# Value products in three blocks per head pair instead of four, and a staggered inversion of the softmax sums

## The chip, the core and the metric

The kernel runs on one core of one Trainium2 chip. The core has a matrix engine (PE, with weight loads shown as PEld), a vector engine (DVE), an activation engine (ACT), a general engine (POOL) and a queue engine (SP) that here issues all DMAs. The metric is the device time of one execution in microseconds (us). Lower is better.

## The reference

One layer over 2048 positions of width 640: a normalized input goes through sliding-window attention (32 heads of width 20, window 256) and, beside it, through a wide layer of 1536 with a squared ReLU; the results are multiplied.

```python
xn = _layernorm(x)                                   # x: 1 x 2048 x 640
qkv = (xn @ wqkv).reshape(B, S, 3, H, Dh)            # H = 32, Dh = 20
scores = einsum("bhqd,bhkd->bhqk", q, k) * Dh**-0.5
mask = (i - j >= 0) & (i - j < 256)
p = softmax(where(mask, scores, -1e9))
s = einsum("bhqk,bhkd->bhqd", p, v) ... @ wo
h = relu(xn @ w1 + b1) ** 2
g = silu(h @ w2 + b2)
return x + s * g
```

## The kernel before

All float32 products are split into a rounded high part and a remainder, and three products of the parts are added up. Contractions over 128 rows of the filler work are cut into two halves of 64 rows, which PE can run side by side on the two halves of its array.

A first stage (to about 139 us) normalizes x, transposes it, and makes the values (v) and the first group of queries and keys. Then comes the main stage: 16 pairs of heads, each with 16 tiles of 128 positions, gives 256 steps and some more at the end (`steps = NP * NT + LAG + PLAG`). A step `s` does, for a pair `p`:

- `scores` (PE, L479; tile `sps`) for tile `s`, from which DVE takes row maxima (L487); every fourth step the maxima of four tiles are turned on PE and sent by a small DMA (`mrow`, L504) into two further rows of the queries `qs`.
- `scores_t` (PE, L519; tile `stps`) for tile `s - LAG` (LAG is 9): the scores transposed, for one tile of keys and the three tiles of queries that see it, with the maximum subtracted through the `mrow` rows; ACT takes the exponential (L525, tile `p`) and POOL clears what lies outside the window (L526, L528). The result stays in one of 8 buffers.
- every fourth step, `values` (PE, L547; tile `ops`): the exponentials of four key tiles times the values, in a block. The last product of a block is PLAG = 2 steps behind its exponentials. A product uses all 128 rows and 32-column strips of the array: two heads and even and odd query tiles in four strips, with 21 columns each, the 21st being a column of ones that gives the softmax sum. The bank `ot` holds four columns of 128, so eight query tiles at a time.
- after a block, `evac` copies two columns to `osb` (ACT, L552) and a DMA stores them (`o<-osb`), 0.8 us later on the planner's clock, into `o_d[g]`, one buffer for each of the four groups `g` of query tiles.

What fills PE between these is one long list of other products, the `filler`: the remaining queries and keys (`qkps`), the wide layer's first product (`hps`) and second (`yps`), and last the output projection (`wops`). `fill` gives out filler until a planner's clock has reached the step's due time; the clock adds a constant for each product (`COST`, and `PV` for a block of values), and `pace` spreads the whole over the steps. DMAs are issued by SP in the order in which the code writes them; loads of x for the wide layer (`xb`), of the next pair's queries and keys, and stores are handed out by `issue` and `post_all` in each step.

The last stage: `wops` needs the attention output divided by the softmax sums. `invert` loads the sums of a group (`rec<-o`, L1064) once the last pair's block has been stored (`stored(g)`), inverts them (DVE, L1066) and stores them (L1067); `load` fetches the outputs (`ob<-o`, L1107) and the inverses (`sums<-rec`, L1108); `turn_out` multiplies them (DVE, L1123) and splits them. `late` calls these in the last blocks of `yps`.

Of the kernel before, what the change touches and what calls it, by code (L numbers as in the profile page):

```python
# [9 lines left out]
F32 = mybir.dt.float32  # L10
F32R = mybir.dt.float32r
BF16 = mybir.dt.bfloat16
AF = mybir.ActivationFunctionType
ALU = mybir.AluOpType

P = 128
# [5 lines left out]
NT = S // P  # L22
KC = D // P
NP = H // 2
NB = 4
BT = S // NB
# [4 lines left out]
HALF = D // 2  # L31
NFH = F // 2 // P
WIDE = 2
FHALF = F // 2
MT = 256
LAG = 9
# [4 lines left out]
WARM2 = 10  # L41
COST = {P: 0.067, 2 * P: 0.12, HALF: 0.147, 3 * P: 0.172, BT: 0.23}
SCALE = DH ** -0.5
PV = 1.57
PLAG = 2
NEG = -1.0e30
EPS = 1e-5
SETTLE = 0.45
# [10 lines left out]
def attn_mlp_kernel(ctx: ExitStack, tc, x, wqkv, wo, w1, b1, w2, b2, out):  # L59
    nc = tc.nc  # L60
# [25 lines left out]
    o_d = [dram.tile([NP, P, MT], F32, name=f"o_{g}") for g in range(NB)]  # L86
# [326 lines left out]
    at2 = ctx.enter_context(tc.tile_pool(name="at2", bufs=2))  # L413
# [9 lines left out]
    clock = [0.0, 0.0, 0.0]  # L423
# [106 lines left out]

    ot = po_.tile([P, 4, P], F32, tag="o", name="ops")

    def values(p, g):
        for kb in range(4 * g, 4 * g + 4):
            pt = pts.pop((p, kb))
            ts = range(kb, min(kb + 3, NT))
            same, other = [t for t in ts if t % 2 == kb % 2], [t for t in ts if t % 2 != kb % 2]
            parts = [same] if kb % 8 < 6 else [[t] for t in same]
            for part in parts + [other]:
                for hh in range(2):  # L540
                    if not part:
                        continue
                    t = part[0]
                    r0 = 32 * (2 * hh + t % 2)
                    c0 = t // 2 % 4
                    first = t % 8 < 2 and kb == max(0, t - 2) or kb == 0
                    nc.tensor.matmul(ot[r0:r0 + VW, c0:c0 + len(part), :], vps[p][:, kb // 4, kb % 4, hh, :], pt[:, hh, :].rearrange("p (t n) -> p t n", n=P)[:, t - kb:part[-1] - kb + 1:2, :], start=first, stop=part[0] == kb, skip_group_check=True)  # L547
        clock[:2] = [max(clock[:2]) + PV] * 2

        def evac():  # L550
            osb = at2.tile([P, 2, P], F32, tag="osb", name="osb")
            nc.scalar.activation(osb, ot[:, 2 * g % 4:2 * g % 4 + 2, :], AF.Copy)  # L552
            post(o_d[g][p], osb.rearrange("p e n -> p (e n)"), 0.8)
        later(SOON, evac)


    state = [0.0, 0.0, 0]
# [3 lines left out]
    def post(dst, src, wait=0.0, then=lambda: None):  # L561
        def go():
            posts.append((dst, src))
            then()
        if whole[0] or not wait:
            go()
        else:
            later(wait, go)

    def post_all():  # L570
        for dst, src in posts:
            nc.sync.dma_start(dst, src)
        posts.clear()
# [9 lines left out]
    def later(wait, fn):  # L583
        tasks.append((clock[0] + wait, len(tasks), fn))
# [274 lines left out]
    def filler():  # L859
# [6 lines left out]
        for g, b in order_qk:  # L866
# [9 lines left out]
            for w in "qk":  # L876
                hi, lo = (t() for t in ws[g][w])
# [35 lines left out]
        def late():  # L913
            j = lates[0]
            lates[0] += 1
            if j >= 3:
                load(0)
            if j >= 4:
                load(1)
            if j >= 6:  # L920
                turn_out(0, 0)
            if j >= 7:
                turn_out(0, 1)
                load(2)
# [120 lines left out]
        return 4 * (u // 2) + u % 2 + 2 * t2  # L1045

    def stored(g):
        return NP * NT - NT + 4 * g + 3 + LAG + PLAG

    rec_d = [dram.tile([2, H, MT], F32, name=f"rec_{g}") for g in range(NB)]  # L1050
    recs = {}

    lates = [0]

    def invert():
        for g in range(NB):
            over = state[2] >= 10 ** 6
            if not over and state[2] < stored(g) + 3:
                return
            if g not in recs:  # L1060
                rows = o_d[g].rearrange("p (h r) n -> (p h) r n", h=2)
                recs[g] = at2.tile([P, P], F32, tag="rec", name="rec")
                for par in range(2):
                    nc.sync.dma_start(recs[g][64 * par:64 * (par + 1)], rows[:, 32 * par + DH].rearrange("h (j n) -> h j n", n=P))  # L1064
            elif recs[g] is not None and (state[2] >= stored(g) + 5 if not over else True):
                nc.vector.reciprocal(recs[g], recs[g])  # L1066
                nc.sync.dma_start(rec_d[g].rearrange("a h (j n) -> (a h j) n", n=P), recs[g])  # L1067
                recs[g] = None

    def room_of(tag, name):  # L1070
        if tag == "p32":
            return at2.tile([P, 2, 3 * P], F32, tag="p32", bufs=8, name=name).rearrange("p a n -> p (a n)")[:, :D]
        return wgt.tile([P, D], F32, tag=tag, name=name)
# [24 lines left out]
    def load(u):  # L1098
        if u in ld or u >= 2 * NB or recs.get(u // 2, 0) is not None:
            return  # L1100
        if u % 2 == 0:
            obs[u // 2] = bigp.tile([P, KC * BT], F32, tag="big", name=f"ob_{u // 2}")
        ob = obs[u // 2][:, u % 2 * 2 * D:(u % 2 + 1) * 2 * D].rearrange("p (c n) -> p c n", c=KC)
        sums = at2.tile([P, MT if u // 2 % 3 == 0 else BT], F32, tag=("sums", "relu", "sq")[u // 2 % 3], name="sums")[:, :MT]
        rows = o_d[u // 2].rearrange("p (h r) n -> (p h) r n", h=2)[:, 32 * (u % 2):32 * (u % 2) + VW]
        for k in range(4):
            nc.sync.dma_start(ob[32 * k:32 * k + H], rows[:, k:DH:4])  # L1107
        nc.sync.dma_start(sums, rec_d[u // 2][u % 2].unsqueeze(0).to_broadcast([4, H, MT]))  # L1108
        ld[u] = (ob, sums)
# [86 lines left out]

    fl = filler()
    steps = NP * NT + LAG + PLAG
    pace = (8 * (KC - 1) * 15 * COST[BT] + 2 * NB * (15 * (WIDE * COST[BT] + 2 * (NFH - WIDE) * COST[MT]) + 8 * 18 * COST[HALF]) + NP * (2 * NT * COST[3 * P] + NB * PV)) / (steps - 1)

    def fill(upto):
        soon()
        while clock[0] < upto:
            c = next(fl, None)
            if c is None:
                clock[0] = upto
                soon()
                return
            if whole[0]:
                clock[:2] = [clock[0] + c] * 2  # L1210
            soon()

    with tc.manual_schedule(engines={E_.PE, E_.Activation, E_.DVE, E_.Pool, E_.SP}):
        load_v(0)
        nc.vector.memset(ot, 0.0)
        loads = []

        def at_step(n):
            return divmod(n, NT) if 0 <= n < NP * NT else None

        for s in range(steps):
            state[2] = s
            vload[0] = 0.2 * (s % 4 == 0) + 0.5 * (s % 4 == 3)
            post_all()
            invert()
            if s >= NP * NT - NT + LAG + 2:
                fetch_y()
            issue(RATE)
            a, b, e = (at_step(s - lag) for lag in (0, LAG, LAG + PLAG))
            if a:  # L1230
                p, q = a
                if q == 0:
                    ensure_bulk(loads)
                if s == 2:
                    ones_rows(1)
                if q == 2 and p < NP - 1:
                    assert made_for(p + 1, 0)
                    loads = [bulk_dma(0.7, *l) for l in pair_loads(p + 1, 0)]
                if q == LAG and p < NP - 1:
                    assert made_for(p + 1, 1)  # L1240
                    loads += [bulk_dma(0.7, *l) for l in pair_loads(p + 1, 1)]
                if q == LAG + 4 and p < NP - 1:
                    load_v(p + 1)
            rows = None
            if a:
                sc = scores(p, q)
            if b:
                stp = scores_t(*b)
            if s % 4 == 0 and 0 < s <= NP * NT:
                rows = max_rows((s - 1) // NT, (s - 1) % NT // 4, stp[0] if b else pair_tile())  # L1250
            if a:
                maxima(*a, *sc)
            if b:
                exps(*b, *stp)
            if rows:
                rows()
            fill((s + EARLY_FILL) * pace)
            post_all()
            issue(RATE)
            flush()  # L1260
            tick()
            if e and e[1] % 4 == 3:
                fill((s + 1) * pace - PV)
                values(e[0], e[1] // 4)
            else:
                fill((s + 1) * pace)
        finish()
        post_all()
        state[2] = 10 ** 6
        for _ in fl:  # L1270
            post_all()
            flush(mark() - 1)
        flush()
        post_all()
# [23 lines left out]
```

## Time and profile before

| | |
|---|---|
| median of 3 runs | 859.34 us (858.82 to 859.89) |
| profiled execution, its own time | 859.53 us |
| its span | 857.8 us |
| granted PE clock, mean | 0.997 |
| DVE, ACT, POOL busy | 54%, 49%, 38% |
| main stage with blocks of values | about 139 to 776 us of the span |
| output projection | 782.9 to 853.5 us |

The profile records one execution. Rows of groups give line, engine, operation, output and inputs with their sizes, the number of instructions, then busy time in us and the mean of one in ns, then the idle time ahead of them with what ended it. Rows of the timeline give start, duration, engine, line and a number of merged instructions. In the trace each value product is two instructions.

### The profile page before, as it was taken

The page shows a single profiled execution, that of the slowest core. Times are in us where ns is not written, and L with a number is a line of the kernel's source. Part 1 is how long each engine was busy: PE and PEld are TensorE (multiplying, and loading weights), DVE is VectorE, ACT ScalarE, POOL GpSimd, SP SyncE. Part 2 cuts the span into 40 slices and gives each one's busy share as a digit, 9 for nine tenths or more (in the row PEclk, how much of TensorE's full clock was granted, in tenths as well). Part 3 has the DMA queues.
Part 4 walks back from the last instruction along what each step waited for, and adds up shares of the span by engine and source line. Part 5 has one row for each costly group of instructions (what it writes and reads, how often), then busy time and mean ns, then how long its engine had stood idle before and what let it go on. Part 6 is the DMA issues. An engine that isn't in the chain of part 4 may idle for free.

```text
span 857.8 us, 25542 instructions
## 1 busy us (share of the span) xinstructions
PE 845.3 (99%) x10160; PEld 786.1 (92%) x10160; DVE 459.1 (54%) x1370; ACT 421.6 (49%) x792; POOL 328.7 (38%) x652
## 2 busy tenths in 40 slices
PE   9999999999999999999999999999999989999998
PEld 8999999888888899999999989999999989999997
DVE  7652136656577545455445466655445444435764
ACT  5222114545556753754654764854754743753321
POOL 6010002334333553553543543643543533541443
PEclk9999999999999999999999999999999999999999
DMA  7997587869889564355266245585376274367992
GB/s 250 327 399 279 170 206 267 263 210 286 278 260 275 146 215 130 84 172 151 77 198 184 61 130 162 144 256 165 77 208 191 61 229 127 126 155 198 277 258 111
DMA packets 94366, 166.42 MB, mean 194 GB/s; under 512 B 10920, under 2 KB 43816, under 8 KB 93224
## 3 DMA queue, kind: packets, MB, share of 16 engines
q1 hardware_dynamic: 94248, 164.80, 63.3%
q8 instruction: 80, 1.31, 0.6%
q14 instruction: 38, 0.31, 0.1%
HBM read 93.66 MB, written 70.52 MB: 191 GB/s over the span
## 4 chain that ended last, share of the span: by engine, by line
PE 93%; DMA 2%; DVE 2%; ACT 1%; issue 1%; SPq 1%; POOL 0%; DVEq 0%
PE hps L469 20%; PE yps L469 20%; PE qkps L469 13%; PE ops L547 10%; PE wops L607 8%; PE vps L229 8%; PE stps L519 5%; PE sps L479 4%; PE qkps L206 3%; PE tps L173 1%; DMA qs<-mrow 1%; DMA qs<-q_d 1%; DMA yin<-y 1%; DVE junk L487 0%; DMA xt<-in_A_x_dram 0%
## 5 line engine op out<-in xcount | busy, mean ns | idle before, releaser
L487 DVE CUSTOM_DVE_ANT_0 junk<-sps,mask 128x384 bf16<-128x384 f32 (+2 forms) x512 | 272.6, 532 | 251.7 <-PE hps L469 70.1
L525 ACT ACTIVATE p<-stps 128x768 f32<-128x768 f32 (+2 forms) x256 | 197.5, 772 | 264.6 <-PE stps L519 216.2
L526 POOL TENSOR_SCALAR_AFFINE_SELECT p<-p 128x256 f32<-128x256 f32 x256 | 107.7, 421 | 332.7 <-ACT p L525 327.8
L469 PE MATMUL yps<-w,hh 64*128 64x320 f32 x1536 | 229.2, 311 | 1.8 <-DVE ysb L996 1.7
L469 PE MATMUL hps<-xb,w 64*128 64x256 f32 (+1 forms) x2100 | 218.6, 305 | 0.0
L469 PEld LDWEIGHTS hps<-xb,w 64*128 64x128 f32 x2100 | 199.2, 187 | 6.2 <-issue 5.1
L469 PEld LDWEIGHTS yps<-w,hh 64*128 64x128 f32 x1536 | 182.2, 186 | 7.5 <-issue 3.4
L469 PE MATMUL yps<-w,hl 64*128 64x320 f32 x768 | 173.5, 310 | 0.0
L479 PE MATMUL sps<-ks,qs 60*128 60x384 f32 (+2 forms) x512 | 141.5, 341 | 1.3 <-DVE mt L487 1.1
L519 PE MATMUL stps<-qs,ks 62*128 62x384 f32 (+2 forms) x512 | 134.5, 332 | 2.4 <-DMA qs<-mrow 2.4
L469 PEld LDWEIGHTS yps<-w,hl 64*128 64x128 f32 x768 | 113.5, 186 | 1.8 <-issue 1.7
L469 PE MATMUL qkps<-xT,wgkh 64*128 64x512 f32 x320 | 100.6, 395 | 0.0
L469 PE MATMUL qkps<-xT,wgqh 64*128 64x512 f32 x320 | 98.1, 392 | 0.0
L528 POOL TENSOR_SCALAR_AFFINE_SELECT p<-p 128x256 f32<-128x256 f32 x224 | 94.1, 420 | 0.0
L547 PE MATMUL ops<-p,vp 128*21 128x128 f32 (+1 forms) x2112 | 92.8, 313 | 0.0
L519 PEld LDWEIGHTS stps<-qs,ks 62*128 62x128 f32 x512 | 87.1, 188 | 3.4 <-issue 2.7
L479 PEld LDWEIGHTS sps<-ks,qs 60*128 60x128 f32 x512 | 85.3, 185 | 4.2 <-DVE mt L487 2.7
L547 PEld LDWEIGHTS ops<-p,vp 128*21 128x21 f32 x2112 | 65.2, 100 | 23.6 <-issue 11.4
L229 PE MATMUL vps<-wv,xT 128*128 128x320 f32 x480 | 71.5, 308 | 0.0
L229 PEld LDWEIGHTS vps<-wv,xT 128*128 128x128 f32 x480 | 70.5, 188 | 0.1
L966 POOL TENSOR_TENSOR hl<-sq,hh 128x512 fp32r<-128x512 f32 x48 | 62.2, 1296 | 19.0 <-ACT sq L965 18.8
L607 PE MATMUL wops<-wo,oT 128*128 128x320 f32 x384 | 61.6, 309 | 0.7 <-DVE ysb L996 0.7
(104 smaller groups left out, 1166.8 us busy)
## 6 DMA issues: line engine op xcount, KB each, us to landing
ks<-k_d SPq DMA_DIRECT2D x64, 240.0 KB
qs<-q_d SPq DMA_DIRECT2D x64, 240.0 KB
xb<-xs SPq DMA_DIRECT2D x60, 256.0 KB
xs<-xT SPq DMA_DIRECT2D x8, 1280.0 KB
k_d<-shm SPq DMA_DIRECT2D x19, 512.0 KB
q_d<-shm SPq DMA_DIRECT2D x19, 512.0 KB
y<-ysb SPq DMA_DIRECT2D x28, 320.0 KB
o<-osb SPq DMA_DIRECT2D x64, 128.0 KB
```

Source lines behind the costliest of these rows:

```text
L206: nc.tensor.matmul(ps, wt[:, c, :], xT[part][b][:, c * BT + t0:c * BT + t0 + n], start=m == 1, stop=m == 3 * KC)
L229: nc.tensor.matmul(ps, xT[xp][b][:, c * BT + t * P: c * BT + (t + 1) * P], wv[wp][:, c, nh * HALF:(nh + 1) * HALF], start=first and m == 0 ...
L469: return nc.tensor.matmul(out, a[r], b_[r], skip_group_check=True, **kw)
L479: nc.tensor.matmul(ss[hh][:, :nk], qs[i][o, q * P:(q + 1) * P], ks[i][o, k0 * P:k0 * P + nk], start=True, stop=True)
L487: nc.vector.tensor_tensor_reduce(out=junk[:, :nk], in0=ss[hh][:, :nk], in1=mask[:, 3 * P - nk:], scale=1.0, scalar=-3.0e38, op0=ALU.add, o ...
L519: nc.tensor.matmul(tps[:, hh, :n], ks[i][o, kb * P:(kb + 1) * P], qs[i][o, kb * P:kb * P + n], start=True, stop=True)
L525: nc.scalar.activation(p32[:, :, :n], tps[:, :, :n], AF.Exp, scale=SCALE)
L526: nc.gpsimd.affine_select(p32[:, :, 0:P], p32[:, :, 0:P], pattern=[[0, 2], [1, P]], compare_op=ALU.is_ge, fill=0.0, base=0, channel_multip ...
L528: nc.gpsimd.affine_select(p32[:, :, 2 * P:], p32[:, :, 2 * P:], pattern=[[0, 2], [-1, P]], compare_op=ALU.is_gt, fill=0.0, base=0, channel ...
L547: nc.tensor.matmul(ot[r0:r0 + VW, c0:c0 + len(part), :], vps[p][:, kb // 4, kb % 4, hh, :], pt[:, hh, :].rearrange("p (t n) -> p t n", n=P ...
L607: nc.tensor.matmul(ps, a, b_, start=j == 0, stop=j == n - 1)
L966: nc.gpsimd.tensor_sub(hh[1][:, :BT], sq, f32(hh[0]))
```

## The change

The 16 key tiles of a pair are cut at 6, 12 and 16 instead of every 4; the blocks stand one step behind the exponentials instead of two, and each has its own cost on the planner's clock. A block's sums leave `ot` as three, three and two columns, in one or two copies where they wrap around, and go to the groups' buffers without the booked delay. In the last stage the inversion takes one group at a time, in one buffer, and waits some calls between its load and the reciprocal; the first loads of outputs start one call later.

```diff
-PV = 1.57
-PLAG = 2
+CUTS = (0, 6, 12, NT)
+PVS = (2.25, 2.25, 1.42)
+PLAG = 1
...
-    def values(p, g):
-        for kb in range(4 * g, 4 * g + 4):
+    def values(p, i):
+        lo, hi = CUTS[i], CUTS[i + 1]
+        for kb in range(lo, hi):
...
-        clock[:2] = [max(clock[:2]) + PV] * 2
+        clock[:2] = [max(clock[:2]) + PVS[i]] * 2
 
         def evac():
-            osb = at2.tile([P, 2, P], F32, tag="osb", name="osb")
-            nc.scalar.activation(osb, ot[:, 2 * g % 4:2 * g % 4 + 2, :], AF.Copy)
-            post(o_d[g][p], osb.rearrange("p e n -> p (e n)"), 0.8)
+            c0, c1 = lo // 2, hi // 2
+            osb = at2.tile([P, 3, P], F32, tag="osb", name="osb")
+            c = c0
+            while c < c1:
+                n = min(4 - c % 4, c1 - c)
+                nc.scalar.activation(osb[:, c - c0:c - c0 + n], ot[:, c % 4:c % 4 + n, :], AF.Copy)
+                c += n
+            for g in range(c0 // 2, (c1 + 1) // 2):
+                d0, d1 = max(c0, 2 * g), min(c1, 2 * g + 2)
+                post(o_d[g][p, :, (d0 - 2 * g) * P:(d1 - 2 * g) * P], osb[:, d0 - c0:d1 - c0].rearrange("p e n -> p (e n)"))
         later(SOON, evac)
...
-            if j >= 3:
+            if j >= 4:
                 load(0)
-            if j >= 4:
                 load(1)
...
     def stored(g):
-        return NP * NT - NT + 4 * g + 3 + LAG + PLAG
+        return NP * NT - NT + min(c for c in CUTS if c >= 4 * (g + 1)) - 1 + LAG + PLAG
...
+    calls, ready = [0], [0]
 
     def invert():
+        calls[0] += state[2] >= 10 ** 6
         for g in range(NB):
             over = state[2] >= 10 ** 6
-            if not over and state[2] < stored(g) + 3:
+            if over and calls[0] < ready[0]:
+                return
+            if not over and state[2] < stored(g) + 2 or over and calls[0] < ready[0]:
                 return
             if g not in recs:
+                if any(r is not None for r in recs.values()):
+                    return
+                ready[0] = calls[0] + 3
...
-                recs[g] = at2.tile([P, P], F32, tag="rec", name="rec")
+                recs[g] = at2.tile([P, P], F32, tag="rec", bufs=1, name="rec")
...
-            elif recs[g] is not None and (state[2] >= stored(g) + 5 if not over else True):
+            elif recs[g] is not None and (state[2] >= stored(g) + 4 if not over else True):
...
                 recs[g] = None
+                ready[0] = calls[0] + 2
...
-            if e and e[1] % 4 == 3:
-                fill((s + 1) * pace - PV)
-                values(e[0], e[1] // 4)
+            if e and e[1] + 1 in CUTS:
+                i = CUTS.index(e[1] + 1) - 1
+                fill((s + 1) * pace - PVS[i])
+                values(e[0], i)
```

More of the change, by code (lines that the diff above doesn't have):

```diff
@@ L1198, in attn_mlp_kernel @@
     steps = NP * NT + LAG + PLAG
-    pace = (8 * (KC - 1) * 15 * COST[BT] + 2 * NB * (15 * (WIDE * COST[BT] + 2 * (NFH - WIDE) * COST[MT]) + 8 * 18 * COST[HALF]) + NP * (2 * NT * COST[3 * P] + NB * PV)) / (steps - 1)
+    pace = (8 * (KC - 1) * 15 * COST[BT] + 2 * NB * (15 * (WIDE * COST[BT] + 2 * (NFH - WIDE) * COST[MT]) + 8 * 18 * COST[HALF]) + NP * (2 * NT * COST[3 * P] + sum(PVS))) / (steps - 1)
     def fill(upto):
```

## The prediction

> **What bounds the kernel now.** I read the page's busy times and chain first, then the list of what PE (the matrix engine) waits for, then the timeline around single blocks of value products.
>
> ```profile
> span 857.8 us, 25542 instructions
> PE 845.3 (99%) x10160; PEld 786.1 (92%) x10160; DVE 459.1 (54%) x1370; ACT 421.6 (49%) x792; POOL 328.7 (38%) x652
> PE 93%; DMA 2%; DVE 2%; ACT 1%; issue 1%; SPq 1%; POOL 0%; DVEq 0%
> ```
>
> PE is busy 99% of the span and holds 93% of the chain that ended last; every other engine is near half. The change adds no matmul and takes none away, so its worth lies in three places: what PE loses around a block of value products, what it waits for, and how the other matmuls pair up. The waits, in the list for PE (us in total, times, longest):
>
> ```profile
> PE stps L519 <- DMA qs<-mrow: 2.4, 1, 2.4
> PE yps L469 <- DVE ysb L996: 1.7, 2, 1.1
> PE sps L479 <- DVE mt L487: 1.1, 3, 0.7
> ```
>
> They are few. One is large; the others are about 3 us together.
>
> **Term 1: sixteen blocks fewer.** Before, a pair of heads has four blocks (products 0-3, 4-7, 8-11, 12-15); after, three (0-5, 6-11, 12-15). On PE, in the first pair, the first block ended after four products:
>
> ```order
> L547 MATMUL ops<-p_1805,vp_1365 21x256 x2
> L547 MATMUL ops<-p_1805,vp_1365 21x128 x2
> L469 MATMUL qkps<-xT_3_959,wgkh_745 128x512
> L479 MATMUL sps<-ks_117,qs_116 128x384 x2
> L519 MATMUL stps<-qs_116,ks_117 128x384 x2
> ```
>
> After the change, on the same engine and place, products 4 and 5 follow directly:
>
> ```order
> L549 MATMUL ops<-p_1803,vp_1365 21x256 x2
> L549 MATMUL ops<-p_1803,vp_1365 21x128 x2
> L549 MATMUL ops<-p_1852,vp_1365 21x256 x2
> L549 MATMUL ops<-p_1852,vp_1365 21x128 x2
> L549 MATMUL ops<-p_1888,vp_1365 21x256 x2
> L549 MATMUL ops<-p_1888,vp_1365 21x128 x2
> L470 MATMUL qkps<-xT_0_174,wgqh_1508 128x512
> ```
>
> The first fence's return to the 64-row matmuls is gone there. What one such leaving and returning costs is read from the timeline of PE at a block (start, duration, instructions) and the duration of a run of 480 equal matmuls of 320 columns:
>
> ```profile
> 309.69 0.41 PE L469 MATMUL yps<-w,hh 64*128 64x320 f32 x2
> 310.03 1.50 PE L547 MATMUL ops<-p,vp 128*21 128x256 f32 x32
> 311.46 0.41 PE L469 MATMUL yps<-w,hh 64*128 64x320 f32 x1
> 311.46 0.44 PE L479 MATMUL sps<-ks,qs 60*128 60x384 f32 x1
> 311.71 0.30 PE L469 MATMUL yps<-w,hl 64*128 64x320 f32 x1
> 311.74 0.34 PE L519 MATMUL stps<-qs,ks 62*128 62x384 f32 x1
> ...
> 782.86 70.64 PE wops L607 x480
> ```
>
> 70.64 / 480 is 0.147 us for 320 columns, so 0.176 for 384. The first row's two matmuls, one on each half of the array, start at 309.69 and (0.41 less a single one's 0.30 later) 309.80; the halves could go on at 309.84 and 309.95, and the block starts at 310.03: 0.19 and 0.08, 0.14 us on the mean. After it the two halves could take their second matmul at 311.61 and 311.64; they take it at 311.71 and 311.74: 0.10 more. So a block costs 0.24 us for changing over. Inside, this block takes 311.46 - 310.03 = 1.43 us for four products, where two products within a block take
>
> ```profile
> 744.53:745.18 0.65, 0.65 (x16) 1.00 0.98 390
> ```
>
> 0.65 us (busy time of these matmuls in that stretch, their number, clock, DMA share, GB/s). Four would be 1.30, so 0.13 more per block goes to its end. Sixteen blocks fewer: 16 x (0.24 + 0.13) = **5.9 us**. Bounds: with the better half's entry 0.08 + 0.10 + 0.13 = 0.31 each, 5.0; with the worse half's 0.19 + 0.10 + 0.13 = 0.42, 6.7.
>
> The Trainium skill's page "TensorEngine Tiling (Array Packing)", section Tiling Modes, says that a change of tiling mode drains the engine; "TensorE: Matmul & The Clock Gate", section Single matmul latency, puts the constant part of a lone matmul at 398 cycles, 166 ns. An estimate from that page, two drains a block, would be 16 x (0.33 + 0.13) = 7.4 us. The rows above say 0.24, and they decide.
>
> **Term 2: the one long wait.** SP (the queue that issues the DMAs), PE, and the clock around it:
>
> ```profile
> 690.09 5.29 SPq L693 DMA_DIRECT2D xb<-xs  x10
> 699.36 1.19 SPq L504 DMA_DIRECT2D qs<-mrow  x2
> ...
> 706.17 0.44 PE L519 MATMUL stps<-qs,ks 62*128 62x384 f32 x2 [2.43 <-DMA qs<-mrow]
> ...
> 695.00:700.00 5.00, 5.00 (x71) 5.00 (x69) 2.92 (x12) 2.21 (x5) 2.19 (x6) 1.00 1.00 342
> 706.00:710.00 4.00, 3.83 (x31) 3.77 (x33) 0.70 (x2) 1.09 (x2) 0.77 (x2) 0.58 0.57 189
> ...
> 701.58 1.50 PE L547 MATMUL ops<-p,vp 128*21 128x256 f32 x32
> 715.71 1.52 PE L547 MATMUL ops<-p,vp 128*21 128x256 f32 x40
> 725.36 1.50 PE L547 MATMUL ops<-p,vp 128*21 128x256 f32 x32
> ...
> ks<-k_d SPq DMA_DIRECT2D x64, 240.0 KB
> xb<-xs SPq DMA_DIRECT2D x60, 256.0 KB
> ```
>
> Ten loads of x, four of q and k and one store of o, 10 x 256 + 4 x 240 + 128 = 3648 KB, went out ahead of the small load of row maxima (mrow) that the next scores need. At the 342 GB/s of the second stretch they take 10.7 us, and 9.3 lie between their first issue and mrow's. PE stood for 2.43 us and ran at 0.58 of its clock for the next four. From block to block took 14.13 us there and 9.65 next door: 4.5 us lost. "TensorE: Matmul & The Clock Gate", Part 1, of the Trainium skill lets the clock fall after an idle window of about 3.4 us; the trace shows it fallen after 2.43. By that rule the term would be the idle time alone, 2.4, and the time 851.2; since the row contradicts it here, it gets no chance of its own.
>
> What stood on SP between the two mrow rows:
>
> ```order
> L504 DMA qs_116<-mrow 2x4x128 x2
> L693 DMA xb_1_12464<-xs_1_73 128x512 x5
> L693 DMA xb_1_12465<-xs_1_77 128x512 x5
> L693 DMA ks_1351<-k_d 60x1024
> L693 DMA qs_1350<-q_d 60x1024
> L572 DMA o_88<-osb 128x256
> L693 DMA ks_1351<-k_d 60x1024
> L693 DMA qs_1350<-q_d 60x1024
> L504 DMA qs_116<-mrow 2x4x128 x2
> ```
>
> And now, at the same two mrows:
>
> ```order
> L505 DMA qs_116<-mrow 2x4x128 x2
> L702 DMA xb_1_12442<-xs_1_77 128x512 x5
> L702 DMA ks_1351<-k_d 60x1024
> L702 DMA qs_1350<-q_d 60x1024
> L581 DMA o_88<-osb 128x256
> L702 DMA ks_1351<-k_d 60x1024
> L702 DMA qs_1350<-q_d 60x1024
> L919 DMA yin<-y_83 128x640
> L581 DMA y_84<-ysb 128x640
> L505 DMA qs_116<-mrow 2x4x128 x2
> ```
>
> Five of the ten x loads have moved ahead of the earlier mrow; a y load and store (320 KB each by their 128 x 640 values) have come in. 5 x 256 + 960 + 128 + 640 = 3008 KB, 8.8 us at 342 GB/s, under the 9.3. I take the wait as gone: **4.5 us**, down to 0 if it stays.
>
> **The parts I cost at nothing.** Products one step earlier: the last product of a block needs its exponentials (ACT, the activation engine) masked (POOL). One such, from the scores to the block that used them:
>
> ```profile
> 757.96 0.34 PE L519 MATMUL stps<-qs,ks 62*128 62x384 f32 x1
> 758.63 0.82 ACT L525 ACTIVATE p<-stps 128x768 f32<-128x768 f32 x1
> 758.33 1.30 POOL L966 TENSOR_TENSOR hl<-sq,hh 128x512 fp32r<-128x512 f32 x1 [0.29 <-ACT sq L965]
> 759.57 0.42 POOL L526 TENSOR_SCALAR_AFFINE_SELECT p<-p 128x256 f32<-128x256 f32 x1
> 759.93 0.42 POOL L528 TENSOR_SCALAR_AFFINE_SELECT p<-p 128x256 f32<-128x256 f32 x1
> 763.87 1.50 PE L547 MATMUL ops<-p,vp 128*21 128x256 f32 x32
> ```
>
> Ready after 760.35 - 757.96 = 2.39 us; the block began after 5.91. One step less takes 9.65 / 4 = 2.41, the larger booking (2.25 for 1.57) another 0.68, and the sixth product starts at least 2 x 0.65 into its block: 5.91 - 2.41 - 0.68 + 1.30 = 4.12 us. Cover left: 1.7 us; without it every block waits (rival C). A block's sums go out with one or two copies on ACT, sixteen more in all:
>
> ```profile
> L552 ACT ACTIVATE osb<-ops 128x256 f32<-128x256 f32 x64 | 24.2, 378 | 1.4 <-PE ops L547 1.4
> ```
>
> At 0.38 us or less each they fit into ACT's idle half. The sixteen added o stores wait on SP for those copies, with no delay booked any more. Loads of x, q, k or y are queued behind them, and steps pass before those are used; where a store shares its step with an mrow, the mrow is issued first.
>
> The filler matmuls are interleaved anew. No row prices how they pair up on the two halves. Against it stand new small waits. The nearest row for either side is the list's 1.7 + 1.1 us: 3 us to the good, 3 to the bad; I take zero.
>
> **The last stage.** SP issues and DVE (the vector engine) work for the first group of sums:
>
> ```profile
> 749.00 0.32 SPq L572 DMA_DIRECT2D o<-osb  x1
> 751.84 1.25 SPq L1064 DMA_DIRECT2D rec<-o  x2
> 755.68 0.33 SPq L1067 DMA_DIRECT2D rec<-rec  x1
> 760.88 0.58 SPq L1108 DMA_DIRECT2D sums<-rec  x1
> 754.70 0.95 DVE L1066 RECIPROCAL rec<-rec 128x128 f32<-128x128 f32 x1 [6.89 <-DMA rec<-o]
> 770.90 1.56 DVE L1123 TENSOR_TENSOR ob<-ob,sums 128x512 f32<-128x512 f32 x2
> ```
>
> A load lands 754.70 - 751.84 = 2.9 us after issue, so the sums were there at 763.8 and used at 770.9: 7.1 us of slack. The first group now ends ten steps ahead of the last step, not twelve, 4.8 us; and behind the last block 28 filler matmuls are left instead of 52, 12 pairs x 0.147 = 1.8. Slack 0.5. On SP before:
>
> ```order
> L572 DMA o_85<-osb 128x256
> L1085 DMA yk_13511<-y_84 128x640
> L504 DMA qs_1350<-mrow 2x4x128 x2
> L1064 DMA rec<-o_85 64x1x128 x2
> L1067 DMA rec_1359<-rec 128x128
> L780 DMA raw<-in_A_wo_dram 32x640 x4
> L572 DMA o_86<-osb 128x256
> L1107 DMA ob_13849<-o_85 32x5x256 x4
> L1108 DMA sums<-rec_1359 128x1x256
> ```
>
> and after:
>
> ```order
> L581 DMA o_85<-osb 128x256
> L581 DMA o_86<-osb 128x128
> L1079 DMA rec<-o_85 64x1x128 x2
> L789 DMA raw<-in_A_wo_dram 32x640 x4
> L1082 DMA rec_1359<-rec 128x128
> L919 DMA yin<-y_83 128x640
> L1123 DMA ob_13869<-o_85 32x5x256 x4
> L1124 DMA sums<-rec_1359 128x1x256
> ```
>
> The weight loads and the next store no longer stand between the inverse's store and its load. That stretch, 755.68 to 760.88, was 5.2 us; the ob loads and the landing need some 3. So slack is 0.5 to 2.7 us, and I take no wait.
>
> **The sum.** Against the profiled execution's 859.5 (its span of 857.8 and 1.7 around it; the median of the three runs, 859.34, is 0.2 lower): 859.5 - 5.9 - 4.5 = **849.1 us**.
>
> **The rivals.** *A: the mrow wait stays* or an equal one comes where other x loads meet an mrow; for it, 8.8 us of transfers is close to 9.3. 859.5 - 5.9 = 853.6. *B: the last stage starves*: sums one group at a time with under 3 us of slack; a slip of 6 us beyond it leaves PE idle for 3 to 6 us: 852 to 855. *C, slower: every block waits for its last exponentials.* If one ACT instruction (0.82) and one on POOL (1.30) stand ahead, they are ready after 2.39 + 2.12 = 4.51 us against 4.12: 0.39 x 48 = 18.7 us, 867.8. It ends slower from 10.4 / 48 = 0.22 us a block on. Against it: in the case shown POOL had such a 1.30 us instruction in hand and lost little. *D: the new interleaving is worth its whole 3 us* : 846.1.
>
> **How the numbers follow.** Forecast 0.60, A 0.20, B 0.07, D 0.06, C 0.07. The forecast's own range is 845.3 to 853.0: term 1 from 5.0 to 6.7, and 3 us either way. To hold 8 in 10 it reaches up through A and most of B: 846 to 855.5. Less than 0.2% (1.7 us) is about what a measurement of this kernel can tell from no change. Forecast, A, B and D lie 4 us or more below; I leave 0.03 of A and B for same. Faster 0.90, same 0.03, slower 0.07.
>
> **What would show it.** Right: 48 blocks, those of six products taking about 1.43 + 0.65 = 2.1 us; no PE row released by mrow near 700 us, and no clock below 1 in the middle; block-to-block sums shorter by some 0.37 us for each block removed. Wrong: PE idle before the value products on POOL, idle ahead of the first output matmul for more than the present 0.7 us, or an mrow wait elsewhere.

## The result, and the profile after

The changed kernel takes **873.04 us** (median of 4 runs, 872.33 to 873.9), the kernel before 859.62 beside it: a ratio of **1.0154** (95% interval 1.0135 to 1.0172). It is 13.4 us slower; 849.1, faster, was forecast. The head of the page of the changed kernel:

```profile
span 871.0 us, 25575 instructions
PE 852.2 (98%) x10160; PEld 795.0 (91%) x10160; DVE 457.2 (52%) x1370; ACT 420.5 (48%) x792; POOL 325.7 (37%) x652
```

Its list of what PE waits for (us in total, times, longest):

```profile
PE wops L616 <- DVE res L1203: 8.2, 2, 5.0
PE sps L480 <- DVE mt L488: 1.5, 7, 0.3
PE yps L470 <- DVE ysb L1004: 1.3, 3, 0.5
```

The wait for mrow has left the list, no row has value products waiting for POOL, and a new row leads: the output matmuls stand for 8.2 us. The output matmuls of the kernel before, by their tile (durations in ns, first and last start):

```profile
L607 PE MATMUL wops<-wo,oT x384: 305/309/383, 782.9 to 852.7; 128*128 128x320 f32 x192
```

The same of the changed kernel:

```profile
L616 PE MATMUL wops<-wo,oT x384: 305/309/634, 781.7 to 866.0; 128*128 128x320 f32 x192
```

I divide the span there. The *main stage* runs from the first scores of the main loop (116.5 us in both) to the first output matmul, the *output stage* from there to the end of the last one. The main stage went from 666.3 to 665.2 us, -1.1 where -10.4 was forecast; the output stage from 70.6 to 85.1, +14.4 where nothing was. The spans differ by the sum of the two, 871.0 - 857.8 = 13.2, to a tenth.

**In the main stage** the blocks are what they were to be. PE at a block of six (timeline; scores and products only):

```profile
439.74 0.34 PE L480 MATMUL sps<-ks,qs 60*128 60x384 f32 x2
442.00 0.34 PE L480 MATMUL sps<-ks,qs 60*128 60x384 f32 x2
444.52 0.34 PE L480 MATMUL sps<-ks,qs 60*128 60x384 f32 x2
445.56 2.17 PE L549 MATMUL ops<-p,vp 128*21 128x128 f32 x56
447.66 0.44 PE L480 MATMUL sps<-ks,qs 60*128 60x384 f32 x1
...
449.29 0.34 PE L480 MATMUL sps<-ks,qs 60*128 60x384 f32 x1
```

447.66 - 445.56 = 2.10 us for six products, as forecast. But scores follow one another after 2.26, 2.52, 3.14 and 1.63 us: the step with the block is long and the next one short. Over all pairs of heads the medians are 3.22 and 3.14 for the two steps with a block of six, 1.68 and 1.62 for those behind them; before, the medians of the 16 steps lay between 2.28 and 2.57. In a short step DVE does not clear the two banks of scores in time. Here a piece of a weight (`w<-raw`, DVE splits the weights piece by piece) stands between its maxima. DVE in the timeline of the changed kernel:

```profile
284.87 0.56 DVE L488 CUSTOM_DVE_ANT_0 junk<-sps,mask 128x384 bf16<-128x384 f32 x1
285.36 0.48 DVE L808 TENSOR_TENSOR w<-raw,w 128x256 fp32r<-128x256 f32 x1
285.76 0.55 DVE L488 CUSTOM_DVE_ANT_0 junk<-sps,mask 128x384 bf16<-128x384 f32 x1
```

And PE in the same stretch, idle ahead of both scores:

```profile
284.78 0.44 PE L480 MATMUL sps<-ks,qs 60*128 60x384 f32 x1 [0.23 <-DVE mt L488]
285.50 0.44 PE L480 MATMUL sps<-ks,qs 60*128 60x384 f32 x1 [0.27 <-DVE mt L488]
```

Gaps in which neither half of PE works and which end in scores came to some 2.0 us in 5 before (PE's timeline of the whole stage, gap by gap) and 4.9 us in 20 after.

**In the output stage** the inverses come late. SP's stores of the last pair's outputs in the kernel before, second and third group:

```profile
758.54 0.34 SPq L572 DMA_DIRECT2D o<-osb  x1
770.70 0.34 SPq L572 DMA_DIRECT2D o<-osb  x1
```

In the changed kernel:

```profile
755.21 1.09 SPq L581 DMA_DIRECT2D o<-osb  x2
772.17 1.08 SPq L581 DMA_DIRECT2D o<-osb  x2
```

Before, groups one to four were stored at 749.0, 758.5, 770.7 and 778.1. After, 755.21 is the first group and half of the second. With cuts at 6 and 12 the second group (products to 7) is complete only with the second block, as is the third (to 11): both at 772.2. The new `stored(g)` says so before any run: it gives the same step for both. One buffer then takes them one after the other. SP in that stretch of the changed kernel:

```profile
790.10 0.55 SPq L1124 DMA_DIRECT2D sums<-rec  x1
799.95 0.34 SPq L1082 DMA_DIRECT2D rec<-rec  x1
807.29 1.20 SPq L1079 DMA_DIRECT2D rec<-o  x2
```

DVE there:

```profile
800.01 1.56 DVE L1139 TENSOR_TENSOR ob<-ob,sums 128x512 f32<-128x512 f32 x2 [7.26 <-DMA ob<-o]
811.89 0.95 DVE L1081 RECIPROCAL rec<-rec 128x128 f32<-128x128 f32 x1 [7.37 <-DMA yk<-y]
```

And PE, at its two stops:

```profile
802.03 3.55 PE L616 MATMUL wops<-wo,oT 128*128 128x320 f32 x12 [3.20 <-DVE res L1203]
813.25 1.97 PE L616 MATMUL wops<-wo,oT 128*128 128x320 f32 x6 [5.01 <-DVE res L1203]
```

The second group's inverses are loaded at 790.10 and used at 800.01. The third's are stored at 799.95, though their reciprocal had run at 787.62: on SP that store stands behind the loads of outputs. The last group's load (807.29) needs the same buffer and waits for that store to land; its reciprocal (811.89; its row names the load of y that SP issued right behind) stands in DVE's order ahead of the products `res` that free the banks of the output matmuls, and PE stands for 5.01 us. The list of the chain that ended last (the work that the last instruction hung on, followed backwards) names both transfers:

```profile
790.10 9.79 DMA sums<-rec
...
799.95 7.27 DMA rec<-rec
```

The two stops are 8.2 of the 14.4 us. The other 6.2 go with the clock, granted at a half behind each stop and at the start of the stage (windows of the changed kernel: busy times, clock, DMA share, GB/s):

```profile
782.00:786.00 4.00, 4.00 (x19) 4.00 (x19) 1.27 (x3) 2.73 (x4) 0.00 (x0) 0.62 0.35 95
802.00:806.00 4.00, 3.97 (x16) 3.97 (x17) 2.53 (x3) 1.71 (x3) 2.12 (x2) 0.57 1.01 280
814.00:818.00 4.00, 4.00 (x17) 4.00 (x17) 4.00 (x5) 2.36 (x4) 2.67 (x3) 0.50 1.08 251
```

At the full clock and 0.147 us each, 27 output matmuls start in 4 us; here it is 19, 16 and 17. Windows cut closer read a clock of 0.50 from 781.60 to 785.02, 802.08 to 805.50 and 812.32 to 819.15 us, 13.6 us of the stage. PE stood in 0.9 of them; half of the rest is 6.3.

### The profile page after: what moved, and what is told of

Its sections match the earlier page's. It is cut to its first block, busy times and chain, and to the rows that moved or that the text cites. A ratio compares the mean times of both kernels' runs of the same rounds, so it can differ in the third digit from the quotient of the medians.

```text
span 871.0 us, 25575 instructions
## 1 busy us (share of the span) xinstructions
PE 852.2 (98%) x10160; PEld 795.0 (91%) x10160; DVE 457.2 (52%) x1370; ACT 420.5 (48%) x792; POOL 325.7 (37%) x652
## 5 line engine op out<-in xcount | busy, mean ns | idle before, releaser
L470 PE MATMUL hps<-xb,w 64*128 64x256 f32 (+1 forms) x2100 | 213.1, 305 | 0.0
L470 PEld LDWEIGHTS hps<-xb,w 64*128 64x128 f32 x2100 | 195.2, 187 | 4.7 <-issue 3.8
L470 PE MATMUL yps<-w,hl 64*128 64x320 f32 x768 | 179.0, 309 | 0.0
L480 PE MATMUL sps<-ks,qs 60*128 60x384 f32 (+2 forms) x512 | 137.0, 341 | 2.1 <-DVE mt L488 1.5
L520 PE MATMUL stps<-qs,ks 62*128 62x384 f32 (+2 forms) x512 | 127.9, 337 | 0.0
L470 PEld LDWEIGHTS yps<-w,hl 64*128 64x128 f32 x768 | 120.2, 185 | 0.9 <-issue 0.9
L480 PEld LDWEIGHTS sps<-ks,qs 60*128 60x128 f32 x512 | 81.2, 185 | 9.8 <-DVE mt L488 7.9
L520 PEld LDWEIGHTS stps<-qs,ks 62*128 62x128 f32 x512 | 79.3, 187 | 0.8
L616 PE MATMUL wops<-wo,oT 128*128 128x320 f32 x384 | 67.2, 328 | 8.9 <-DVE res L1203 8.2
L616 PEld LDWEIGHTS wops<-wo,oT 128*128 128x128 f32 x384 | 62.6, 204 | 9.6 <-DVE res L1203 8.7
```

The source lines that it names most:

```text
L470: return nc.tensor.matmul(out, a[r], b_[r], skip_group_check=True, **kw)
L480: nc.tensor.matmul(ss[hh][:, :nk], qs[i][o, q * P:(q + 1) * P], ks[i][o, k0 * P:k0 * P + nk], start=True, stop=True)
L520: nc.tensor.matmul(tps[:, hh, :n], ks[i][o, kb * P:(kb + 1) * P], qs[i][o, kb * P:kb * P + n], start=True, stop=True)
L616: nc.tensor.matmul(ps, a, b_, start=j == 0, stop=j == n - 1)
```

## The experiments

Medians are of all runs of a kernel on its chip, ratios against the kernel before on the same chip, stages of the one profiled execution of each.

| kernel | median us | ratio (95%) | main stage | output stage |
|---|---|---|---|---|
| before | 859.62 | 1 | 666.3 | 70.6 |
| changed | 873.04 | 1.0154 (1.0135 to 1.0172) | 665.2 | 85.1 |
| blocks_only | 863.09 | 1.0042 (1.0025 to 1.0058) | 666.1 | 74.4 |
| tail_only | 863.83 | 1.0050 (1.0031 to 1.0070) | 667.5 | 74.0 |
| fours_one_behind | 862.00 | 1.0028 (1.0012 to 1.0043) | 667.4 | 70.6 |
| no_calls | 871.75 | 1.0149 (1.0107 to 1.0191) | 666.2 | 81.9 |
| two_at_a_time | 865.63 | 1.0068 (1.0049 to 1.0087) | 666.7 | 76.5 |
| no_early_fill | 860.83 | 1.0009 (0.9992 to 1.0026) | 660.3 | 74.7 |
| fours_no_early_fill | 859.17 | 0.9985 (0.9966 to 1.0005) | 664.6 | 70.6 |
| even_and_moved | 856.16 | 0.9965 (0.9947 to 0.9983) | 657.9 | 75.8 |
| pieces_moved | 867.80 | 1.0092 (1.0068 to 1.0117) | 669.2 | 76.3 |
| after_even | 862.90 | 1.0034 (1.0021 to 1.0047) | 665.1 | 73.3 |
| early_inverse | 853.84 | 0.9934 (0.9912 to 0.9956) | 664.6 | 70.6 |

**The change in two halves.** *blocks_only* is the changed kernel with the inversion and load order of before (up to two groups in hand):

```diff
+            if j >= 3:
+                load(0)
...
-            if not over and state[2] < stored(g) + 2 or over and calls[0] < ready[0]:
+            if not over and state[2] < stored(g) + 3:
...
-                if any(r is not None for r in recs.values()):
-                    return
-                ready[0] = calls[0] + 3
```

The second buffer, for groups two and four, is one of the values' buffers.

> The changed kernel's blocks (six, six, four products, one step behind) with the inversion and the load order of the kernel before. The last stage of the changed kernel took 14.4 us longer (85.07 us for the 480 output matmuls against 70.64), its main stage 1.2 us less. Theory, one-at-a-time inversion: the 14.4 us go, the output matmuls take about 71 us and the whole 873.0 - 14.4 = 858.6 us. Rival, later blocks: the last stage starves because the last blocks end closer to it, whatever the inversion does; the output matmuls stay at 80 to 85 us and the whole at 868 to 873.

*tail_only* is the kernel before with the changed `invert` and `late` and nothing else.

> The kernel before with its blocks of four, and only the changed inversion (one group at a time, one buffer, calls between its parts, first loads one call later). Theory, one-at-a-time inversion: output matmuls 80 to 85 us, the whole 859.6 + 10 to 14 = 869 to 874, with the third group's sums and the last group's reciprocal waited for. Rival, later blocks: output matmuls 71 us, the whole 859 to 861.

Neither theory had the whole of it. The old inversion takes 10.7 of the 14.4 us off (85.1 to 74.4), but 3.8 us stay with the blocks; the new one alone costs 3.4. Together they cost 14.4, twice the 7.2 of their sum: the single buffer hurts where two groups become ready together. In tail_only it is mostly the clock: the first 48 output matmuls take 9.83 us, 7.11 in the kernel before. Its list of waits and one of its windows:

```profile
PE wops L607 <- DVE ysb L995: 1.1, 1, 1.1
PE wops L607 <- DVE res L1194: 0.2, 1, 0.2
```

```profile
786.00:790.00 4.00, 4.00 (x17) 4.00 (x17) 1.58 (x3) 1.42 (x3) 0.18 (x1) 0.50 1.00 311
```

**One step behind, by itself**: the kernel before with `PLAG = 1`.

> The kernel before with one number changed: the products stand one step behind the exponentials, not two; blocks stay at four. If the one step costs nothing, as the prediction took it: 858 to 861, the main stage at 666 us. Rival, the missing 9 us of the main stage come from the one step: 865 to 869, main stage 672 to 676, with PE idle before the value products.

Not the 9 us, though not free: 1.7 us by the medians. In its list the wait for mrow is down from 2.4 to 0.2 us, and another has taken its place (1.7 before); none is for the value products. In this one profile the step costs more than the medians show: the main stage is 667.4 us against 666.3, although the mrow wait and the half clock behind it, 4.1 us in the kernel before, are all but gone.

```profile
PE yps L469 <- DVE ysb L996: 4.6, 4, 2.3
```

**Calls or buffer.** *no_calls* sets the two waits of the changed inversion to one call and none; *two_at_a_time* keeps the three calls and has two buffers.

```diff
-                ready[0] = calls[0] + 3
+                ready[0] = calls[0] + 1
...
-                ready[0] = calls[0] + 2
+                ready[0] = calls[0]
```

> The changed kernel with its one buffer and one group at a time, but without the calls between the parts of the inversion: the reciprocal follows the load in the next call, the next load the store in the next. In the changed kernel the third group's inverses were stored at 799.95 us and the last group's reciprocal ran at 811.89; without the calls their instructions stand ahead of the loads of outputs again. Theory, the waiting calls: the output matmuls fall from 85 us to 74 to 77 and the whole to 862 to 865. Rival, the single buffer: store and load of the groups still follow one another, the output matmuls stay at 82 us or more and the whole at 870 or more.

```diff
-                if any(r is not None for r in recs.values()):
+                if sum(r is not None for r in recs.values()) > 1:
...
-                ready[0] = calls[0] + 3
+                ready[g] = calls[0] + 3
```

> The changed kernel with two buffers and up to two groups in hand, but with the three calls between a group's load and its reciprocal kept. Groups two and three become ready in the same step, so they are now loaded and inverted together. Theory, the single buffer: output matmuls 74 to 77 us, the whole 862 to 865. Rival, the waiting calls: the last group's reciprocal still stands behind its three calls; output matmuls 78 to 85, the whole 866 to 873.

The buffer. Without the calls the stage keeps 81.9 us; the chain of one buffer only shows elsewhere, as one stop of 6.05 us where the last group's reciprocal waits for its load in DVE's order. SP of no_calls:

```profile
787.36 0.37 SPq L1082 DMA_DIRECT2D rec<-rec  x1
793.39 1.17 SPq L1079 DMA_DIRECT2D rec<-o  x2
```

DVE of no_calls:

```profile
796.33 0.95 DVE L1081 RECIPROCAL rec<-rec 128x128 f32<-128x128 f32 x1 [7.89 <-DMA rec<-o]
```

With two buffers and the calls kept, it is 76.5 us and 7.4 us less by the medians. What the calls and the later first loads each have in the 2.1 us that are left to blocks_only (74.4), no run separates.

**Uneven steps.** *no_early_fill* is blocks_only, and a step with a block gives out no filler ahead of it:

```diff
-            fill((s + EARLY_FILL) * pace)
+            if not (e and e[1] + 1 in CUTS):
+                fill((s + EARLY_FILL) * pace)
```

> The kernel of blocks_only, but a step with a block gives out no filler ahead of its block (before: up to 0.4 of a step). Steps with a block took 3.14 to 3.22 us and the next 1.62 to 1.68 in the changed kernel, and the scores waited 20 times for the maxima, 4.9 us, where they waited 5 times, 2.0 us, before. Theory, uneven steps: the scores' waits fall to about 2 us, and the main stage by 3 to 9 us against blocks_only. Rival, the booked clock does not matter: waits and main stage within 1.5 us of blocks_only.

*fours_no_early_fill* does the same to the kernel before, for `e[1] % 4 == 3`.

> The kernel before (blocks of four, two steps behind) where a step with a block gives out no filler ahead of its block. Control for no_early_fill, which took 2.3 us (medians) off the kernel with long blocks. If that came from the long blocks' uneven steps, the short blocks have little to win: 858 to 861, the same as before. Rival, filler ahead of a block is a loss of itself: 855 to 857, as much off as with the long blocks.

The steps with and behind a block of six become 2.62 to 2.66 and 2.08 to 2.12 us. The scores' row in the list of waits falls from 1.8 us (6 times, blocks_only) to

```profile
PE sps L480 <- DVE mt L488: 0.7, 2, 0.4
```

and the gaps ahead of scores from 5.3 us in 21 to 2.1 in 11. By the medians it is 2.3 us; the profiled execution shows 5.8 in the main stage, but it was the fastest of ten. With blocks of four the medians move by 0.35 us, within what is measured: filler ahead of a block does little harm where the block is short.

**Pieces.** In blocks_only with or without the early filler, the steps in which weight pieces are held back from DVE are moved behind the long blocks:

```diff
-            vload[0] = 0.2 * (s % 4 == 0) + 0.5 * (s % 4 == 3)
+            vload[0] = 0.2 * (s % 4 == 0) + 0.5 * (s % 16 in (0, 6, 10))
```

> The kernel of blocks_only (863.1 us, main stage 666.1) with only the steps changed in which weight pieces are held back from DVE: those behind a long block (0, 6 and 10 of 16) instead of every fourth; the filler ahead of a block stays. If the pieces are a cause of their own: the scores' waits fall from 5.3 us in 21 to under 3, the main stage by 2 to 4 us, the whole 859 to 861. Rival, they matter only where the steps are even: within 1 us of blocks_only.

> The kernel of no_early_fill, and the steps in which weight pieces are held back from DVE are those behind a long block (0, 6 and 10 of 16) instead of every fourth. Theory, pieces and maxima meet: the remaining waits of the scores (0.7 us in the list) and of the second products (1.9) shrink by a half, the whole 858 to 860. Rival, nothing: 860.8 as no_early_fill, within 1 us.

With even steps it brings 4.7 us more by the medians (3.8 by the ratios), more than I expected; the profiled execution (at its median) has a main stage of 657.9, 8.2 under blocks_only. Alone it is 4.7 slower (4.3 by the ratios), which neither theory said; the scores' row in its list stays (1.9 us, 5 times). There the first group's outputs and inverses were 4.4 us late, in its list of waits:

```profile
PE yps L470 <- DVE ysb L1005: 6.0, 3, 4.4
```

and on DVE:

```profile
772.97 1.56 DVE L1132 TENSOR_TENSOR ob<-ob,sums 128x512 f32<-128x512 f32 x2 [6.34 <-DMA o<-osb]
```

DVE waits in its order for the first outputs and sums, and the second products (`yps`) behind it stand. Without that stop its main stage is 669.2 - 4.4 = 664.8. The stop is also followed by half clock (0.50 from 772.78 to 779.61 us, PE busy for 4.63 of these 6.83), another 2.3; an estimate without both is 662.5, 3.6 under blocks_only, so the pieces may help alone as well. On SP, four loads of weights (761.35) stand there ahead of the loads of the first outputs, which go out 11.1 us behind these outputs' store (764.52 after 753.40); in blocks_only it is 6.3 (762.86 after 756.61). No run shows that this order is the whole of the delay.

**The changed kernel with the even main stage**: the two edits of even_and_moved, its own inversion kept.

> The changed kernel with its own inversion, and the two edits of even_and_moved in the main stage. Is the loss of the last stage (14.4 us) independent of the main stage? If it is a fixed length of the chain of stores and loads behind the output matmuls: main stage 8 us shorter, output matmuls 83 to 85 us, the whole 864 to 866. Rival, the distance counts: with the blocks of even_and_moved the last block ended 10.5 us ahead of the output matmuls instead of 4.8, so the inversion gets 5 to 6 us of it, output matmuls 78 to 80, the whole 859 to 861.

The distance counts, but part of the loss has only moved. The output stage is 73.3 us, and the main stage 665.1, 7.2 longer than in even_and_moved: 4.6 us of a stop for the first group, as above, the rest half clock behind it (0.50 from 771.01 to 777.84 us). The whole, 862.9, lies between the two. By the ratios the changed inversion costs 0.69% with even steps (against even_and_moved) and 1.12% with uneven ones (against blocks_only), 5.9 and 9.6 us. The list of waits:

```profile
PE yps L470 <- DVE ysb L1004: 4.6, 1, 4.6
PE wops L616 <- DVE res L1203: 0.9, 1, 0.9
```

**Earlier inverses.** In even_and_moved groups two and three are still inverted only at the first output matmul. Its DMA engines nearly idle there (window of even_and_moved, the DMA share last but one):

```profile
774.00:778.00 4.00, 3.63 (x25) 3.66 (x26) 4.00 (x7) 2.73 (x4) 0.21 (x1) 1.00 0.12 41
```

and its DVE waits for what they could have brought:

```profile
788.81 1.56 DVE L1132 TENSOR_TENSOR ob<-ob,sums 128x512 f32<-128x512 f32 x2 [4.88 <-DMA ob<-o]
```

*early_inverse* loads and inverts one step sooner, and goes on while the second products run out:

```diff
-            if not over and state[2] < stored(g) + 3:
+            if not over and state[2] < stored(g) + 2:
...
-            elif recs[g] is not None and (state[2] >= stored(g) + 5 if not over else True):
+            elif recs[g] is not None and (state[2] >= stored(g) + 4 if not over else True):
...
+            turns[0] += 1
+            if not whole[0] and turns[0] % 24 == 0:
+                invert()
```

> The kernel of even_and_moved (856.2 us, output matmuls 75.8 us); groups two and three are inverted one step earlier, at the last step, and the last group while the last second products still run, not after the first output matmuls. There SP issued nothing from 770.6 to 776.6 us and the DMA share was 0.12 from 774 to 778, while DVE later waited 4.9 and 5.5 us for outputs and inverses. Theory, late inverses: the output matmuls fall to 71 to 72 us, the whole to 851 to 853. Rival, the DMA engines are simply full from 782 us on (share 1.0): the same bytes have to pass, output matmuls 74 to 76, the whole 855 to 857.

The output stage is 70.6 us again, with no stop in it; the whole is just above the 851 to 853 expected. The bytes were not the bound, and what the old inversion left with the long blocks (3.8 us in blocks_only, 5.2 in even_and_moved) was its late start. Both groups are inverted at 768.08, 13 us ahead of the first output matmul (DVE):

```profile
768.08 2.03 DVE L1075 RECIPROCAL rec<-rec 128x128 f32<-128x128 f32 x2 [1.60 <-DMA rec<-o]
```

Of the 5.2 us some 2.1 go back to the main stage. The reciprocals now stand in DVE's order ahead of the first group's products, PE waits 1.4 us for the second products (at 774.58), and from the last value product to the first output matmul it takes 12.6 us, 10.5 in even_and_moved. In its list of waits stands

```profile
PE stps L520 <- DMA qs<-mrow: 3.5, 2, 2.2
```

It is the fastest of all, 0.66% under the kernel before. The profiled execution was the slowest of its six (857.81). Its main stage is 6.7 us longer than that of even_and_moved, and besides those 2.1 this row accounts for it: mrow again, twice, at 223 and 391 us, 2.9 us more than in even_and_moved (0.6), the same program up to there, and 1.7 for 3.41 us at half clock behind the first.

## Why the prediction was wrong

- **Term 1, sixteen blocks fewer**: right as far as it can be counted: 48 blocks, 2.10 us for six products. Over all blocks of PE's timeline, the time from a block's first product to the next other matmul sums to 88.3 us before and 86.2 after, 2.1 less, as 16 x 0.13 has it; the gaps ahead of the blocks, worked out as in the prediction, fall from 8.3 to 6.6 us, 1.7 for its 2.2. The 0.10 us behind a block was not counted. With even steps, a hidden output stage and blocks of either length, 853.84 (early_inverse) stands against 859.17 (fours_no_early_fill); as ratios to the kernel before 0.9934 and 0.9985, 0.5% or some 4.4 us. These two also differ in the pieces and in mrow waits, so 5.9 is not measured alone.
- **Term 2, the long wait**: gone from the changed kernel's profile as forecast. In the kernel before it was worth 4.1 us for the forecast 4.5: 2.43 of waiting and half of the 3.41 us at half clock behind it (706.64 to 710.05). But it is not gone for good: it comes back in another kernel with the same blocks (early_inverse, 3.5 us). Rival A described a margin, not a place, and the margin was thinner than the prediction has it: the profile's KB are 1024 bytes (60 x 1024 floats are listed as 240.0 KB), so 3008 KB take 9.0 us, not 8.8, of the 9.3.
- **"The filler matmuls are interleaved anew ... 3 us to the good, 3 to the bad; I take zero"**: the first step that failed. The main stage fell short by 9 of the 10.4 us, three times its bound, since the bound was read from the waits of a kernel whose steps were even. The numbers for it lay open: a step is about 2.4 us, early filler fills 0.4 of it, and a block books 2.25 behind that, 0.4 x 2.4 + 2.25 = 3.2 us; 3.22 and 3.14 were measured. I used the larger booking only for the cover of the exponentials. Making the steps even and moving the pieces took the main stage to 657.9, 8.4 below before of the 10.4 forecast. The gaps ahead of the scores are only 2.9 of the 9 us. An estimate from PE's timeline, at 0.147 us for 320 columns, for the rest: from the changed kernel to even_and_moved the time with neither half at work falls by 5.8 us, 4.2 of them ahead of scores, and the time with one half alone by 2.6.
- **"The last stage ... I take no wait"**: the second step that failed, and the larger. I followed the first group alone. Its slack (0.5 to 2.7) was enough in the changed kernel, but not in pieces_moved and after_even, where PE stood 4.4 and 4.6 us for it. The loss lay in the groups behind it: two complete in one store, one buffer for both. Rival B had the mechanism, but with a slip of 6 us and a stop of 3 to 6; it was 8.2 us of stops and 6.2 of half clock, 14.4. The sign set for it, more than 0.7 us idle ahead of the first output matmul, did not show (0.7 as before): the stops came 17 and 27 us later.
- **Products one step earlier and rival C**: the cover held, as the sum had it; no value product waited for its exponentials in the list of the changed kernel. One step behind cost blocks of four 1.7 us in other waits, more in its profile, so a part of the 9 us above may be its; even_and_moved, which has it too, leaves room for some 2. Rival C, the only slower one, did not happen. The kernel was slower by a way to which I had given a faster time.

## What to carry to other kernels

When pieces of work are made longer, lay them on the schedule's clock first: a piece that overruns its step shortens the next, and whatever serves the scarce buffers in the short step becomes the wait. When blocks are cut anew, ask for every consumer which cut now completes it; two that become ready together need two buffers, and a chain of store, load and store through memory has to start while the transfer queues are still idle. Slack must be followed for the last link of such a chain, not the first.

## What the hardware showed that I had not expected

Small dependent transfers stretch when the DMA engines are full. The 9.79 and 7.27 us above, from issue to landing (128 and 64 KB), fell in windows with a DMA share of mostly 0.9 to 1.1. The first group's load of sums (two of 32 KB) had landed 2.9 us after its issue in the kernel before, at a share of 0.24.

The granted clock falls on the same instructions in one kernel and not in another. The changed kernel and blocks_only both run 4.2 us with one half of PE and stop for 0.68 us ahead of the output matmuls; the first 12 of these took 3.33 us in the one and 1.83 in the other, where the window reads

```profile
782.00:786.00 4.00, 3.36 (x23) 3.39 (x24) 4.00 (x7) 2.64 (x4) 0.00 (x0) 1.00 0.94 316
```

The Trainium skill's page "TensorE: Matmul & The Clock Gate", Part 1, says that the activity window runs freely, so that the moment of a change depends on where in it the work falls. These two runs agree with that. The window's length of about 3.4 us shows too: from the first scores to the last output matmul, nine of the thirteen profiles have stretches at half clock, and each lasts 3.41 or 6.83 us. That a whole window must be idle does not show here: a stop of 0.68 us behind half use was enough in the one kernel and not in the other, and 2.43 us in the kernel before. Whether the half use counts in it, no run shows.
